# Two new tables for a fused attention, expert and convolution kernel: one for the order of its work, one for the engine of each step

## The chip, the cores and the metric

The kernel runs on one core of a Trainium2 chip. The metric is device time in microseconds (us), from one launch to its end. The core has TensorE (matmuls, written PE in the profile, with its weight loads as PEld), VectorE (DVE), ScalarE (ACT), GpSimd (POOL) and SyncE (SP), which here only issues DMA transfers.

## The reference

Three layers follow each other, on a batch of 4 with 576 positions. Local attention has 8 heads of 64; beside a band of 7 neighbours, each head attends over positions pooled by 4. A layer of 4 experts with causal attention follows, of which every token takes the best 2. Last is a gated convolution.

```python
# attention: q, k, v of shape (4, 8, 576, 64)
out_d = sm_attn(mean of q by 4, mean of k by 4, mean of v by 4)   # 144 x 144 scores
out_up = np.repeat(out_d, 4, axis=2)
scores = scale * q @ k.T where abs(i - j) < 4, else -1e9
out = out_up + softmax(scores) @ v
# experts: x of shape (4, 576, 512)
topk, w = best 2 of x @ w_gate, softmax over them
for e in range(4):
    a = softmax(causal(scale * (x @ wq[e]) @ (x @ wk[e]).T))
    out += (gate of e) * (a @ (x @ wv[e]) @ wo[e])
# gated convolution
gate = sigmoid(sum over k of conv_w[k] * shifted(x, k))           # 5 taps
return (gate * (x @ w_val)) @ w_out
```

## The kernel before

All of the work is cut into **pieces**. A piece belongs to one engine, issues one or a few instructions there, and names the buffers that it reads and writes. There are 2773 numbered pieces, 321 of which fall away by a choice of engine; 636 of the rest are TensorE's, 810 VectorE's, 566 ScalarE's, 305 GpSimd's and 135 are transfers. For each of the 4 batches these come one after another:

- `attention(b)`: for each of 4 pairs of heads the loads `qt`, `kt`, `vw`, `v`; the sums by 4 that give `qd` and `kd` (lines 946 and 953); pooled scores (1083), transposes (1099) and values (1117); band scores (1142, 1148), transposes (1161, copied out to `pT` at 1168) and values (1183). `softmax` is shared by both: the largest of each row (1007), its scaling `mx` (1017), the exponentials on ScalarE with a read of their accumulator (1022) or without one and a sum on VectorE after it (1028 and 1042), a small step `sm` that adds an epsilon (1051, 1053 or 1055 by engine), the reciprocal (1059) and the product with it (1068, 1070). The pooled values are scaled to `od` (1125), their transposed weights are copied to `pdT` (1106). The result x is split into a high and a low half, `xh` (798) and `xl` (815).
- `project(b)`: products of x with `wvg` (values `vE` and gate logits) and `wqk`, each as three matmuls of halves, all on lines 1228 to 1230. `experts(b)`: scores (1380, 1392), least score (1407, 1410), exponentials (1419), weighting by gate and sum (`weigh`, 1484 to 1520, where `rf` at 1510 is the product of two columns), transposes (1441, 1458), values (1552).
- `tail(b)`: the convolution (1600 to 1614) and the last products, again on lines 1228 to 1230, then scaling (1646, 1648) and the store.

Weights are loaded and split once; `w_val` and `w_out` come as 64-bit numbers and are decoded by lines 854 to 875, `w_val` is first multiplied by `wo` on TensorE (896). There are eight banks of PSUM (`ps`), shared by all stages, with a cap for each kind of use.

Nothing is issued in the order in which it is written down. `Plan.order()` walks through all pieces with costs and delays of its own and takes, for each engine that is free, the ready piece with the least **due time** for which there is room; the list that results is the program's order, fixed before it is compiled. The due time of a piece is `DUE[idx]`, with `idx` its number. A due time is a priority: the pieces that are ready are sorted by it, and no engine waits for a clock. Pieces of VectorE and GpSimd that are marked "port" are kept apart by the walk where a small delay allows it.

Which engine takes a step is a second table. Every step that more than one engine can do calls `pick` with its options, and the n-th call is answered by the n-th digit of `PICK`; a step that needs a helper on another engine (a copy out of PSUM for GpSimd, `rf` for ScalarE) gets it through `same`.

```python
def pick(self, name, *options):
    n = len(self.picks)
    k = min(int(PICK[n]), len(options) - 1) if n < len(PICK) else 0
...
p = Piece(engine, cost, late, (DUE[idx] if idx < len(DUE) else 0.0, idx), fn, k, size)
...
form = pick("a_" + key, *forms)             # ("act", "dve", ["none",] "pool", "half", "halfp")
tiny = pick("m_" + key, "act", "dve", "pool")
norm = pick("n_" + key, "act", "dve", "pool")
en = pick("pt_%s%d" % (key, c), "act", "dve")
```

Of the kernel before, what the change touches and what calls it, by code (L numbers as in the profile page):

```python
# [34 lines left out]
    0.3, 1.5, 0.7, 5.45, 1.6, 0, 0.15, 3.85, 3.6, 5.2, 4.58, 0.5, 6.19, 2, 3.88, 4.83, 0, 1, 9.28, 4.5,  # L35
    16.58, 3.52, 4.1, 6.05, 6.81, 0.5, 1.5, 6, 22.88, 5, 4.59, 5.08, 6.73, 7.22, 17.54, 18.54, 7.78,
    10.77, 11.82, 12.71, 12.29, 12.29, 14.5, 15.06, 15.35, 10.26, 11.2, 11.67, 11.89, 12.93, 14.04,
    14.63, 14.92, 16.62, 18.95, 18.53, 21.15, 22.48, 24.1, 12.93, 15.14, 15.84, 16.3, 16.3, 15.74,
    15.74, 16.3, 18.4, 19.77, 19.98, 15.54, 16.14, 16.14, 16.14, 16.3, 18.17, 19.37, 20.11, 20.98,
    21.27, 22.24, 23.25, 23.67, 24.3, 25.31, 25.72, 29.93, 30.84, 26.62, 27.82, 28.67, 29.8, 19.93,  # L40
    21.38, 22.41, 22.86, 22.88, 21.98, 21.98, 22.88, 24.96, 26.51, 26.86, 21.77, 22.37, 24.74, 22.81,
    22.37, 22.37, 22.81, 26.84, 27.4, 27.62, 28.69, 30.31, 30.41, 31.47, 32.48, 32.71, 33.81, 34.55,
    32.6, 35.41, 36.28, 37.2, 14.58, 16.08, 25.52, 29.42, 29.92, 19, 19.57, 22.52, 23.1, 21.38, 21.88,
    26.02, 33.48, 32.48, 26.15, 28.09, 27.07, 28.76, 38.08, 39.1, 25.08, 26.61, 27.49, 28.05, 27.82,
    27.2, 27.2, 27.82, 30.15, 32.11, 32.82, 27, 29.09, 30.66, 29.47, 27.6, 27.6, 29.47, 33.14, 33.4,
    33.62, 30.15, 31.59, 32.53, 33, 32.99, 34.03, 35.12, 36.22, 36.51, 32.2, 33.65, 34.31, 34.31, 35.7,
    36.42, 37.11, 37.42, 39.01, 40.64, 40.64, 43.37, 45.19, 45.36, 41.49, 42.74, 43.77, 44.96, 46.38,
    46.38, 47.01, 47.83, 46.38, 46.81, 47.39, 47.9, 34.03, 36.31, 37.91, 38.37, 38.41, 36.91, 36.91,
    39.9, 40.54, 41.15, 41.44, 36.71, 38.34, 38.81, 42.74, 37.31, 37.31, 44.12, 44.72, 45.59, 45.88,
    47.39, 48.66, 49.08, 49.87, 50.88, 51.19, 52.95, 53.68, 50.88, 50.88, 51.49, 51.88, 8.78, 16.41,  # L50
    16.83, 2.5, 7.96, 8.58, 4, 14.11, 14.72, 2, 7.58, 8.04, 23.38, 32.18, 34.17, 3, 8.93, 9.66, 22.38,
    29.18, 30, 15.08, 19.59, 20.38, 0, 6.42, 6.65, 6.88, 6.19, 5.5, 3.5, 10.65, 11.27, 11.42, 11.89,
    12.43, 13.81, 14.7, 18.02, 17.08, 15.58, 21.3, 21.85, 22.17, 22.9, 23.64, 25.02, 27.4, 25.97, 35.97,
    26.52, 39.99, 39.44, 41.24, 41.71, 42.79, 44.52, 50.65, 48.22, 62.46, 68.35, 72.56, 73.44, 73.47,
    74.01, 74.55, 75.98, 76.87, 79.31, 78.06, 0, 79.68, 80.5, 0, 81.49, 25.02, 31.29, 36.67, 28.92,
    38.23, 39.56, 91.07, 95.14, 95.28, 95.87, 96.51, 97.05, 98.35, 98.89, 98.73, 103.73, 104.59, 104.68,
    105.49, 106.54, 108.62, 110.24, 111.36, 45.41, 54.53, 55.08, 55.3, 56.23, 56.77, 58.25, 59.13,
    59.78, 59.13, 63.3, 63.85, 64.07, 64.78, 65.52, 67.02, 70.22, 70.96, 76.87, 81.7, 82.25, 82.63,
    84.21, 85.88, 87.59, 90.08, 91.52, 65.82, 66.18, 66.54, 66.9, 68.83, 68.15, 61.71, 62.07, 63.23,
    65.46, 66.35, 67.23, 57.48, 57.84, 58.2, 58.56, 60.29, 61.81, 53.46, 53.82, 54.54, 55.79, 56.81,  # L60
    60.56, 31.01, 38.28, 49.42, 54.18, 56.96, 54.82, 69.17, 69.57, 68.61, 69.91, 71.18, 71.73, 69.39,
    69.77, 72.45, 73.28, 73.82, 74.35, 74.87, 75.46, 80.78, 86.85, 69.38, 72.38, 72.73, 73.09, 73.99,
    74.54, 67.77, 68.23, 68.58, 69.73, 70.76, 70.32, 71.4, 73.44, 73.8, 74.15, 74.51, 75.65, 77.73,
    62.43, 63.59, 63.95, 65, 65.69, 65.69, 66.69, 35.55, 40.41, 52.92, 55.34, 59.18, 59.75, 58.94,
    59.51, 56.57, 57.15, 68.94, 70.09, 70.53, 71.83, 73.12, 72.61, 75.06, 54.9, 56.15, 56.59, 57.03,
    59.74, 62.55, 60.61, 62.88, 60.01, 62.31, 60.28, 60.83, 61.27, 62.79, 64.72, 64.4, 66.76, 7.44,
    7.33, 75.07, 76.67, 77.37, 76.94, 77.71, 78.06, 78.66, 78.55, 79.15, 79.82, 80.28, 80.55, 81.28,
    80.55, 81.83, 80.55, 81.43, 80.55, 82.35, 84.81, 86.38, 86.94, 89.84, 91.58, 92.29, 94.55, 95.43,
    99.19, 81.02, 82.36, 82.87, 82.09, 83.22, 83.81, 86.47, 85.07, 87.06, 87.75, 88.6, 88.88, 89.98,
    89.28, 90.6, 88.88, 90.96, 88.88, 89.22, 92.83, 94, 93.62, 94.92, 96.19, 96.19, 96.85, 97.13, 98,  # L70
    87.32, 88.67, 91, 89.38, 91.73, 94.37, 95, 95.27, 96.2, 95.27, 97.18, 98.5, 99.23, 99.31, 91.95,
    93.13, 94.48, 93.87, 95.52, 97.22, 99.77, 100.05, 103.44, 100.05, 101.53, 106.64, 109.82, 107.8,
    93.33, 96.78, 95.07, 98.53, 99.11, 99.6, 101.15, 104.61, 105.42, 105.83, 106.13, 107.27, 108.59,
    110.76, 113.29, 117.58, 117.19, 118.22, 111.81, 114.29, 116.07, 113.17, 116.63, 117.9, 119.75,
    120.02, 120.76, 120.02, 120.12, 125.38, 127.44, 126.58, 116.85, 117.91, 119.34, 118.65, 120, 121.41,
    121.93, 122.23, 124.79, 122.13, 124.17, 128.2, 129.16, 128.95, 118.11, 122.42, 119.38, 123.13,
    123.62, 126.11, 126.96, 127.71, 128.18, 128.46, 128.46, 129.82, 130.39, 131.42, 133.4, 135.96,
    135.96, 136.76, 32.98, 33.98, 40.59, 54.73, 61.46, 42.03, 43.17, 45.21, 45.72, 34.97, 35.47, 40.09,
    60.96, 61.96, 46.71, 47.61, 49.91, 50.48, 51.61, 52.74, 46.15, 48.26, 48.85, 49.2, 49.2, 48.85,
    48.85, 49.2, 51.29, 52.61, 53.33, 49.51, 50.11, 51.07, 50.56, 50.11, 50.11, 50.56, 53.19, 54.92,  # L80
    58.55, 51.61, 54.04, 54.69, 57.22, 55.02, 55.02, 60.22, 61.1, 62.84, 53.53, 54.56, 55.63, 54.89,
    54.89, 61.19, 61.72, 62.28, 64.3, 65.23, 65.84, 75.86, 77.3, 77.51, 67.26, 69.88, 70.2, 77.83,
    78.83, 78.95, 80.31, 82.86, 78.83, 79.38, 79.93, 80.8, 58.92, 60.08, 60.68, 60.68, 60.68, 61.32,
    61.92, 63.12, 65.04, 65.75, 66.04, 61.91, 63.2, 68, 63.67, 62.51, 62.51, 63.67, 70.62, 71.09, 72.2,
    80.27, 81.01, 81.35, 81.92, 82.93, 83.38, 84.3, 85, 82.93, 83.08, 83.92, 87.12, 48.12, 47.62, 54.23,
    78.83, 79.33, 57.39, 60.48, 55.04, 56.01, 59.96, 60.46, 53.73, 82.93, 90.57, 64.41, 64.98, 68.25,
    68.81, 61.02, 77, 70.97, 72.77, 75.58, 76.04, 76.05, 76.05, 77.97, 78.46, 79.24, 72.25, 73.03,
    74.25, 73.37, 73.37, 75.85, 77.2, 78.17, 83.58, 84.55, 85.47, 86.19, 88.31, 91.56, 78.61, 80.75,
    82.8, 83.27, 83.56, 81.35, 81.35, 85.98, 86.92, 87.41, 87.7, 80.35, 81.15, 84.59, 81.48, 80.95,
    80.95, 81.48, 86.99, 87.5, 88.89, 91.08, 92.56, 92.71, 93.95, 95.15, 95.44, 96.46, 97.23, 95.15,  # L90
    96.2, 96.84, 98.35, 88.42, 90.56, 91.16, 91.16, 91.16, 91.91, 92.9, 94.6, 96.85, 97.51, 97.8, 91.18,
    91.78, 91.78, 91.78, 92.31, 93.26, 97.6, 99.11, 99.84, 100.7, 102.31, 103.05, 103.39, 104.34,
    105.35, 105.93, 106.8, 107.4, 105.45, 105.91, 107.78, 110.42, 97.26, 99.82, 100.44, 100.41, 101.05,
    100.41, 101.84, 100.41, 102.63, 100.41, 103.82, 105.14, 103.63, 103.98, 106.69, 107.49, 108.42,
    96.42, 99, 100.08, 99.69, 100.66, 99.69, 101.45, 99.69, 102.24, 99.69, 103.03, 104.28, 105.93,
    106.28, 107.03, 108.28, 109.26, 107.6, 108.06, 109.88, 109.53, 110.46, 108.65, 111.84, 111.08,
    112.6, 108.91, 113.29, 114.12, 109.84, 110.56, 114.89, 115.77, 116.29, 95.96, 99.46, 101.63, 100.79,
    102.3, 100.05, 103.42, 100.05, 104.21, 100.05, 105.02, 105.69, 105.12, 105.57, 106.36, 107.18,
    108.08, 119.93, 121, 121.71, 122.06, 123.64, 127.92, 120.64, 121.35, 122.9, 123.25, 123.91, 124.39,
    118.51, 118.87, 119.22, 119.58, 120.16, 134.13, 117.66, 120.29, 126.69, 127.14, 127.81, 139.32,  # L100
    137.86, 138.3, 138.98, 138.98, 139.61, 138.98, 140.2, 138.98, 140.79, 138.98, 141.38, 144.24,
    146.75, 151.2, 152.12, 152.72, 153.41, 130.16, 138.75, 141.12, 139.43, 141.84, 139.43, 142.43,
    139.43, 144.18, 140.72, 145.44, 146.6, 154.55, 154.99, 155.72, 156.65, 157.73, 139.56, 140.01,
# [1609 lines left out]
```

## Time and profile before

| what | value |
|---|---|
| median of 3 runs | 355.61 us (353.96 to 356.92) |
| the profiled execution | 357.07 us |
| its span, first to last instruction | 355.4 us |
| instructions | 11539 |
| mean granted clock of TensorE | 0.974 |
| bytes moved | 31.70 MB, 89 GB/s over the span |

The profile is of one execution. Its span lies within its time, and what is left of the time is ahead of the first instruction and behind the last. Busy times are unions of an engine's instructions. [...]

### The profile page before, as it was taken

The numbers are of one execution on the slowest core, as the hardware profiler recorded it, in microseconds if no ns is written. First come the engines' busy times: TensorE is split into PE (matmuls) and PEld (weight loads), VectorE is DVE, ScalarE is ACT, GpSimd is POOL, SyncE is SP. The second block draws the span as 40 slices with busy tenths as digits, with TensorE's granted clock in tenths as the row PEclk, the third lists the DMA queues.
The fourth block names the chain that finished last, engine by engine and source line by source line (L and its number), as shares of the span: only waits on it lengthen the run. The fifth ranks groups of instructions, "written<-read, shape, count | busy, mean of one in ns | idle before, by whom it ended". The sixth has DMA issues, their size and how long they took to land.

```text
span 355.4 us, 11539 instructions
## 1 busy us (share of the span) xinstructions
PE 332.9 (94%) x4360; PEld 290.8 (82%) x4360; DVE 297.4 (84%) x921; ACT 257.8 (73%) x923; POOL 204.7 (58%) x325
## 2 busy tenths in 40 slices
PE   0697899998999999999999999999999999999996
PEld 0464679876698898999898897998998899997896
DVE  6898998899999899988989786898887668799572
ACT  3778968689888987688786797466765565688462
POOL 7357867559879852477978432384673036444070
PEclk9999589997899999999999999999999999999999
DMA  7979948519431344236222110101000100001022
GB/s 264 258 217 236 235 137 184 155 61 195 110 85 50 91 123 113 52 107 169 65 91 68 50 51 2 39 4 70 9 0 5 44 0 17 0 4 57 15 65 74
DMA packets 26279, 31.70 MB, mean 89 GB/s; under 512 B 2672, under 2 KB 18032, under 8 KB 26224
## 3 DMA queue, kind: packets, MB, share of 16 engines
q1 hardware_dynamic: 26224, 30.97, 32.4%
q8 instruction: 34, 0.56, 0.7%
q14 instruction: 21, 0.17, 0.2%
HBM read 26.24 MB, written 4.72 MB: 87 GB/s over the span
## 4 chain that ended last, share of the span: by engine, by line
PE 81%; DVE 9%; POOL 4%; ACT 3%; issue 2%; POOLq 0%; DVEq 0%
PE ps L1228 19%; PE ps L1229 17%; PE ps L1230 17%; PE ps L1552 7%; PE ps L1380 5%; PE ps L1441 3%; PE ps L1183 2%; PE ps L1148 2%; PE ps L896 2%; PE ps L1117 1%; PE ps L1161 1%; PE ps L1083 1%; DVE mx L1007 1%; ACT p L1022 1%; PE ps L1099 1%
## 5 line engine op out<-in xcount | busy, mean ns | idle before, releaser
L1419 ACT ACTIVATE pe<-ps,mmin 128x128 f32<-128x128 f32 (+4 forms) x80 | 41.9, 527 | 15.3 <-DVE mmin L1410 10.0
L1612 POOL TENSOR_TENSOR row<-row,row 128x256 f32<-128x256 f32 (+1 forms) x40 | 32.0, 804 | 33.0 <-ACT row L1607 18.4
L1614 DVE SCALAR_TENSOR_TENSOR row<-ps,cw,row 128x320 f32<-128x320 f32 (+1 forms) x88 | 43.3, 513 | 6.2 <-ACT row L1600 4.3
L1228 PE MATMUL ps<-gh,wout_h 128*128 128x256 f32 (+1 forms) x128 | 39.3, 307 | 0.5 <-DVE pT L1168 0.5
L1230 PE MATMUL ps<-xh,wqk_l 128*128 128x256 f32 (+1 forms) x128 | 37.8, 295 | 2.1 <-POOL wqk_l L815 2.1
L1228 PE MATMUL ps<-xh,wqk_h 128*128 128x256 f32 (+1 forms) x128 | 39.1, 306 | 0.6 <-DVE vE L790 0.3
L1229 PE MATMUL ps<-gl,wout_h 128*128 128x256 f32 (+1 forms) x128 | 37.8, 295 | 0.0
L1229 PE MATMUL ps<-xl,wqk_h 128*128 128x256 f32 (+1 forms) x128 | 37.8, 295 | 0.0
L1230 PE MATMUL ps<-gh,wout_l 128*128 128x256 f32 (+1 forms) x128 | 37.7, 294 | 0.0
L1552 PE MATMUL ps<-mp,vE 128*64 128x320 f32 (+4 forms) x224 | 27.0, 374 | 0.0
L1230 PEld LDWEIGHTS ps<-xh,wqk_l 128*128 128x128 f32 x128 | 24.2, 189 | 2.3 <-POOL wqk_l L815 2.3
L1228 PEld LDWEIGHTS ps<-gh,wout_h 128*128 128x128 f32 x128 | 24.1, 188 | 2.5 <-POOL gl L815 0.8
L1228 PEld LDWEIGHTS ps<-xh,wqk_h 128*128 128x128 f32 x128 | 24.1, 189 | 2.2 <-DVE vE L790 0.6
L1520 POOL TENSOR_SCALAR pe<-pe,rs,gw 128x128 f32<-128x128 f32 (+3 forms) x31 | 21.0, 683 | 7.8 <-DVE mmin L1415 4.9
L1007 DVE TENSOR_REDUCE mx<-ps 128x5 f32<-128x320 f32 (+1 forms) x48 | 23.7, 519 | 1.1 <-PE ps L1148 0.6
L1229 PEld LDWEIGHTS ps<-gl,wout_h 128*128 128x128 f32 x128 | 24.1, 188 | 0.2 <-POOL gl L815 0.2
L1229 PEld LDWEIGHTS ps<-xl,wqk_h 128*128 128x128 f32 x128 | 24.2, 189 | 0.0
L1230 PEld LDWEIGHTS ps<-gh,wout_l 128*128 128x128 f32 x128 | 24.1, 188 | 0.0
L1228 PE MATMUL ps<-wvg_h,xh 128*128 128x260 f32 (+1 forms) x80 | 23.5, 293 | 0.6 <-POOL xh L798 0.6
L1552 PEld LDWEIGHTS ps<-mp,vE 128*64 128x64 f32 (+1 forms) x224 | 14.2, 138 | 11.9 <-issue 3.9
L1230 PE MATMUL ps<-wvg_h,xl 128*128 128x260 f32 (+1 forms) x80 | 22.7, 284 | 1.0 <-DVE xl L815 1.0
L1229 PE MATMUL ps<-wvg_l,xh 128*128 128x260 f32 (+1 forms) x80 | 22.6, 282 | 0.0
(231 smaller groups left out, 1208.8 us busy)
## 6 DMA issues: line engine op xcount, KB each, us to landing
qt<-in_qT_dram SPq DMA_DIRECT2D x16, 288.0 KB, 3.7
kt<-in_kT_dram SPq DMA_DIRECT2D x16, 288.0 KB, 4.4
v<-in_vx_dram SPq DMA_DIRECT2D x16, 288.0 KB, 5.3
vw<-in_vx_dram SPq DMA_DIRECT2D x16, 192.0 KB, 4.1
out_dram<-o SPq DMA_DIRECT2D x16, 160.0 KB, 1.8
raw<-in_w_val_dram SPq DMA_DIRECT2D x4, 512.0 KB, 5.1
vw<-in_vx_dram SPq DMA_DIRECT2D x16, 128.0 KB, 3.9
raw<-in_w_out_dram SPq DMA_DIRECT2D x4, 512.0 KB, 3.5
```

The lines of the kernel that those rows point to most:

```text
L896: nc.tensor.matmul(pw[m].t, t.t[:, m * P:(m + 1) * P], f.t, start=(c == 0), stop=(c == KC - 1))
L1007: nc.vector.tensor_reduce(out=mx.t[:n, :g, 1], in_=sv(), op=ALU.max, axis=AX.X)
L1228: nc.tensor.matmul(p, ah, bh, start=first, stop=False)
L1229: nc.tensor.matmul(p, ah, bl, start=False, stop=False)
L1230: nc.tensor.matmul(p, al, bh, start=False, stop=last)
L1380: nc.tensor.matmul(s.t[:, o:o + P * (t + 1)], a.t[r, P * t:P * t + P], z.t[r, :P * (t + 1)], start=(k == 0 and t == T[0]), stop=(k == 2 an ...
L1419: nc.scalar.activation(pe.t[:, off + c0:off + c1], s.t[:, o:o + c1 - c0], AF.Exp, bias=m.t[:, 0:1], scale=-1.0, accum_out=sums.t[:, a:a + ...
L1441: nc.tensor.transpose(pt.t[:, i:i + 64], pe.t[r, j * P:(j + 1) * P], ident[r, r])
L1520: ENG[en].tensor_scalar(v, v, x, y, op0=ALU.mult, op1=ALU.mult)
L1552: nc.tensor.matmul(av.t[64 * e:64 * e + 64, z:n], vE.t[:kr, j, 2 * pr + e, :], pT.t[:kr, e, k0:k0 + n - z], start=(j == 0), stop=(j == Tl))
L1612: nc.gpsimd.tensor_add(g.t[:, :nn], g.t[:, :nn], g2.t[:, :nn])
L1614: nc.vector.scalar_tensor_tensor(g.t[:, :nn], x2.t[:, k:k + nn], cw.t[:, m, k:k + 1], g.t[:, :nn], op0=ALU.mult, op1=ALU.add)
```

## The change

Only the two tables change. `DUE` has 2773 entries before and after, so that every piece keeps its number and gets another priority. `PICK` has 1008 digits before and after, and 443 of them differ. The functions that make the pieces, `Plan.order()` and its costs, and all parameters stay. [...] The first and the last lines of `DUE` stand for the rest of it.

```diff
--- before.py
+++ after.py
@@ -32,238 +32,239 @@
 DUE = (
-    0.3, 1.5, 0.7, 5.45, 1.6, 0, 0.15, 3.85, 3.6, 5.2, 4.58, 0.5, 6.19, 2, 3.88, 4.83, 0, 1, 9.28, 4.5,
-    16.58, 3.52, 4.1, 6.05, 6.81, 0.5, 1.5, 6, 22.88, 5, 4.59, 5.08, 6.73, 7.22, 17.54, 18.54, 7.78,
...
-    343.71, 340.39, 343.49, 346.58, 347.02, 347.7, 348.24, 341.72, 343.04, 344.37, 344.81, 345.49,
-    346.02, 340.83, 342.6, 343.93, 345.25, 345.93, 346.53, 339.95, 342.16, 345.7, 346.14, 346.81, 347.35,
+    0.3, 1.8, 0.7, 5.35, 0, 0.5, 0.65, 1.6, 5.95, 6.65, 1.85, 0.8, 6.19, 0, 1.9, 4.15, 0, 1, 6.5, 4.5,
+    16.95, 3.52, 4.64, 4.59, 6.2, 1.5, 2, 5, 21.14, 7, 5.66, 6.39, 6.74, 7.23, 16.12, 17.39, 7.65, 9.7,
...
+    338.9, 340.67, 343.63, 344.23, 344.81, 341.99, 343.32, 344.65, 345.98, 346.65, 347.3, 341.55,
+    343.76, 344.21, 345.53, 346.2, 346.8, 342.44, 342.88, 345.09, 346.42, 347.09, 347.8, 341.11, 346.86,
+    347.3, 347.75, 348.42, 348.96,
 )


 PICK = (
-    "011100000001230000010112021100012002032101000120010100100011231130040010001000000150042211001021"
-    "212000102110110000002121012101010100110000111000010000010000001111000000000100111111120211000001"
-    "001011102000101100222011001010001001003203201021101111010210012000120002102100100101110222121110"
-    "400100010010012202220000012000000100000110110110000000100000000001000011200000010000100011111000"
-    "100111001110010100101010010010101012110112122001002000101101201012011112010001011110110111322002"
-    "100132251111101121202220000010010111111010421420222020000000001121212221000110011001210001210111"
-    "110000200000010020000021000021000021101000101100010001110000110010010110011011001001210101111021"
-    "101011220000110011111211012211001010100101010120222130210011011100110140052211001011110100111152"
-    "130201102011010000012132101101011110001021110010101100010010001111110100002101110001000000110110"
-    "110100011101010010111011000010100000011022112010011100010022101001002110002000120100010000001110"
-    "110010002110010011010000210000211111200100000010"
+    "010100000032210001001202021100012012030100000100000100000031231142040001010101100152040201021021"
+    "010111002110112000002101210110010000010111010001001100000010001010000011000100111111110011000001"
+    "000210001000021100212101011010111101000010014200220100000210212204120002102100000001112000021000"
+    "420010000010012202120000002100102100000000100100110100100000010001000001211100200000101110100010"
+    "011000001100110101110010111101102111100002021000002111101200100012000110000010100111111111022322"
+    "010141150201101120202322001010111101000111202400020221000100001110210221111010210000201000201100"
+    "011000210010001001010001000020010000010111110100100010111010101010110110100000010111200110110022"
+    "201000201102001000110211112010020000100011101000240130042001001001100030041210000001111111101142"
+    "240042141101100012010141050110111120100120000111010021011101010101102001112011000100002000011001"
+    "000110111001111111100011111100100000110022002110111001001010100110101001102201110100011000110010"
+    "000000000100102101100100210010211100010100000110"
 )
```

## Rows read from the trace of the kernel before

**Rows 1.** The page: busy time of each engine, share of the span, instructions.

```profile
PE 332.9 (94%) x4360; PEld 290.8 (82%) x4360; DVE 297.4 (84%) x921; ACT 257.8 (73%) x923; POOL 204.7 (58%) x325
```

**Rows 2.** Windows: length; busy PE, PEld, DVE, ACT, POOL (instructions); clock; DMA share; GB/s.

```profile
0.00:50.00 50.00, 33.57 (x586) 23.87 (x587) 43.28 (x118) 34.37 (x147) 32.52 (x68) 0.90 0.89 237
50.00:100.00 50.00, 47.65 (x685) 39.37 (x685) 46.05 (x155) 42.68 (x176) 38.28 (x52) 0.93 0.54 132
100.00:150.00 50.00, 50.00 (x670) 45.08 (x670) 45.96 (x138) 41.62 (x147) 31.62 (x48) 1.00 0.34 87
...
300.00:355.40 55.40, 52.19 (x457) 46.75 (x456) 38.55 (x112) 33.21 (x91) 19.67 (x28) 0.99 0.11 37
```

**Rows 3.** Waits of TensorE: for whom, us in total, times, longest; last row after 95 us.

```profile
PE ps L1083 <- POOL kd L953: 8.1, 1, 8.1
PE ps L896 <- DVE o L875: 3.2, 1, 3.2
PE ps L1230 <- POOL wqk_l L815: 2.1, 1, 2.1
...
PE ps L1228 <- DVE pT L1168: 0.5, 1, 0.5
```

**Rows 4.** The window from 94 to 352 us, columns as in rows 2.

```profile
94.00:352.00 258.00, 257.47 (x3181) 232.66 (x3176) 214.00 (x673) 185.99 (x625) 138.54 (x215) 1.00 0.18 52
```

**Rows 5.** Timeline of TensorE near 108 us: start us, us, engine, line, operation.

```profile
107.14 0.28 PE L1229 MATMUL ps<-al,wv_h 128*128 128x256 f32 x1
107.26 0.28 PE L1230 MATMUL ps<-ah,wv_l 128*128 128x256 f32 x1
107.47 0.71 PE L1441 MATMUL ps<-ident,pe 64*128 64x64 f32 x16
...
108.42 0.39 PE L1228 MATMUL ps<-ah,wo_h 128*128 128x260 f32 x1
108.64 0.28 PE L1229 MATMUL ps<-al,wo_h 128*128 128x260 f32 x1
```

**Rows 6.** The page: the chain that ended last, shares of the span.

```profile
PE 81%; DVE 9%; POOL 4%; ACT 3%; issue 2%; POOLq 0%; DVEq 0%
```

**Rows 7.** Windows ahead of and in both half-clock stretches, columns as in rows 2.

```profile
26.60:36.84 10.24, 7.02 (x131) 4.40 (x129) 9.09 (x27) 8.24 (x41) 8.17 (x13) 1.00 1.04 236
...
36.84:47.08 10.24, 9.09 (x156) 7.51 (x154) 9.64 (x19) 7.96 (x29) 8.47 (x10) 0.50 0.84 220
...
84.63:91.45 6.82, 6.72 (x93) 5.02 (x93) 6.37 (x23) 6.82 (x33) 6.51 (x10) 0.50 0.69 120
```

**Rows 8.** Groups by shape, VectorE and ScalarE: busy us, mean ns; then idle before.

```profile
L1042 DVE TENSOR_REDUCE sm<-p 128x5 f32<-128x320 f32 x19 | 9.0, 475 | 1.0 <-ACT p L1037 0.8 <-ACT p L1028 0.2
L1168 DVE COPY pT<-ps 128x348 f32<-128x348 f32 x15 | 7.4, 508 | 0.3 <-PE ps L1161 0.3
...
L1106 DVE COPY pdT<-ps 112x432 f32<-112x432 f32 x10 | 5.9, 596 | 0.0
L946 DVE TENSOR_TENSOR row<-kt 128x288 f32<-128x288 f32 x9 | 4.3, 475 | 0.0
L790 DVE COPY vE<-ps 128x256 f32<-128x256 f32 x9 | 3.8, 417 | 0.1
L1125 DVE TENSOR_SCALAR od<-ps 128x144 f32<-128x144 f32 x7 | 2.0, 299 | 0.2
...
L1022 ACT ACTIVATION_READ_ACCUMULATOR p<-ps,mx 128x1 f32 x65 | 14.7, 225 | 0.0
...
L1168 ACT COPY pT<-ps 128x348 f32<-128x348 f32 x17 | 7.3, 461 | 2.7 <-PE ps L1161 2.7
```

**Rows 9.** Instructions of three lines: count, then min/median/max ns, first and last start.

```profile
L1059 DVE RECIPROCAL sm<-sm x48: 147/178/192, 14.4 to 243.5; 128x5 f32<-128x5 f32 x32, 128x3 f32<-128x3 f32 x16
...
L1053 DVE TENSOR_REDUCE sm<-sm x11: 124/149/166, 14.3 to 243.3; 128x5 f32<-128x10 f32 x7, 128x3 f32<-128x6 f32 x4
...
L1510 DVE TENSOR_TENSOR rf<-rs,gw x15: 119/159/686, 89.4 to 329.4; 128x1 f32<-128x1 f32 x15
```

426 rows, old and new, of the table DUE are left out of this document.

## Prediction

> **What bounds the kernel now.** I read the page's busy times first, and they mislead: TensorE looks busy for 94% of the span and VectorE for 84%, as if there were one limit throughout [rows 1]. The windows of 50 us split it. In the first two, TensorE has 16.4 and 2.4 us of idle time, while VectorE is busy for 43.28 and 46.05 of 50 us and the DMA engines for 0.89 and 0.54 of theirs; from 100 us on TensorE has none, and the other engines have more and more of it [rows 2]. The waits of TensorE alone, asked for once from 20 to 95 us and once from 95 to 352 us, give the date of the turn: after 95 us a single wait of 0.5 us stands, and the long ones (2.1 us for the low half of a weight) lie ahead of it; the two longest of all are 8.1 us at the start and 3.2 us for the first decoded weight [rows 3]. The window from 94 to 352 us has 257.47 us of TensorE in 258.00 [rows 4]. A busy TensorE need not be at its peak, so its pace is read from the timeline: matmuls of 256 columns start 0.12 us apart, without a gap, also where a group of transposes stands between them [rows 5].
>
> So the time is three parts: about 94 us in which TensorE is fed too thinly, 258 us that are its own instructions one behind another, and some 3 us at the end in which the last results are scaled and stored (it is busy for 52.19 of the last 55.40 us) [rows 2]. The instructions of the 258 us are the same products whatever their order. **What a new order can win lies in the first 94 us**: how much TensorE work gets done there. The chain of waits says who holds it: outside TensorE it is VectorE 9%, GpSimd 4% and ScalarE 3%, which is 32, 14 and 11 us of 355.4, and since TensorE alone fills the time after 95 us, nearly all of it lies ahead [rows 6]. [...]
>
> **The change part by part.** No instruction of the program is written anew; 443 of the 1008 choices of engine differ, and the order. The digit at place n answers the n-th call of pick(), so each changed digit is a named step, and a mean duration from the groups by shape prices it on either engine.
>
> (a) Work per engine. Over the whole run VectorE loses 6.1 us, ScalarE gains 3.0 and GpSimd 0.5. That would be too coarse a sum, since it counts VectorE where TensorE hides it. Of the steps that stood before 100 us, VectorE loses 3.5 us, ScalarE gains 1.3, GpSimd loses 0.4. The main terms for VectorE: four copies of pT go to ScalarE (4 x 508 ns = 2.03 us), three of od (3 x 299 = 0.90), two of vE (2 x 417 = 0.83), one of pdT (0.60); against them two more sums of exponentials (475 ns for a wide one, the pooled one is longer: 1.07 us in all) and two more pair sums (2 x 475 = 0.95); the rest comes to -1.2 in small items [rows 8]. For ScalarE the four pT copies cost 4 x 461 = 1.84 us, but eight exponentials lose their accumulator read (8 x 225 = 1.8 us) because VectorE now sums them [rows 8]. How much of the 3.5 us reaches TensorE? None, if the loads hold this stage: the DMA share is 1.04 just ahead of 36.84 us [rows 7]. All of it, if VectorE does: 46.05 of 50 us. By the chain, a third (32 of some 95 us), 1.2 us. I take half, **-1.8 us**, because from 50 us on VectorE is the fullest engine but for TensorE and the DMA engines have room; the ends are 0 and -3.5. ScalarE and GpSimd come to about nothing: ScalarE gains 2.5 us before 50 us, where it is busy for 34.37 of 50, and loses 1.2 us in the next 50 [rows 2]: 11% of chain on +1.3 us is **+0.1 us**.
>
> (b) The order on TensorE. Sorted by their due times, 88 of its 636 pieces keep their place and 32 move by over 20 places; the stages stay where they were. The number of changes between kinds of matmul grows from 147 to 151. One such change costs what the start-to-start times show: 0.21 us from the last 256-column matmul to the first transpose, and the group behind starts late in like manner, against 0.12 us within a run [rows 5], so 0.1 us each, **+0.4 us**, and nothing hides it in the 258 us.
>
> (c) The queue of loads. 28 of 135 keep their place. At the start q0, q1, k0, k1 become q0, k0, q1, k1, and the first pair sum of k0 moves from GpSimd to VectorE (475 ns there) [rows 8]. TensorE's first matmul needs kd, the end of that line [rows 3]; but the sums of both pairs now queue on VectorE, and k1 lands last as before. Bounds -0.3 and +0.3 us, I take 0. Among the later loads those of the second weight and of the next batch are exchanged; the cover is the long lead that they have, and what it costs where that is gone is a wait such as the 2.1 us one.
>
> [...]
>
> Sum: -1.8 + 0.1 + 0.4 = -1.3 us. The profiled execution took 357.07 us, 1.7 us more than its span of 355.4, and the median of the three runs is 355.61; the same difference gives 355.8 for the one and **354.3 us** for the other, -0.4%.
>
> **The rivals.** First, nothing is gained: the loads hold the first 40 us and the freed VectorE time waits for them. For it: the DMA share of 1.04. Against it: the share is 0.54 from 50 to 100 us. It gives 355.6 + 0.4 = 356.0 us. [...]
>
> Second, faster by over 1%: the half-clock stretch at 84.63 us goes, because with VectorE freed TensorE has no thin stretch ahead of it. It would give 354.3 - 3.4 = 350.9 us; with all of the 3.5 us, 349.2. Against it: nothing in the tables aims at that place, and the pooled transposes and a band stage move up there by 2 to 4 us of due time, which can thin it as well.
>
> Third, slower: TensorE is fed too thinly before 47.08 us and the first half-clock stretch lasts once more as long. ScalarE has 2.5 us more to do before 50 us, and most of what TensorE works on there passes through it first. Another 10.24 us at half clock cost up to 5.1 us, and with no gain of VectorE that is 356.0 + 5.1 = 361.1; another 6.82 us give 359.4. It decides from the point at which the rise at 47.08 us comes later than about 54 us. Against it: ScalarE keeps over a quarter of that window idle.
>
> **How the numbers follow.** Forecast 354.3, from 352.3 with (a) and (c) at their low ends to 355, where the next case begins: 0.42. Nothing gained, 355 to 357: 0.21. The clock stretch gone, 349 to 352: 0.21. Slower, 357.5 to 361: 0.16. About 1%, 3.6 us, is what a measurement of this kernel can tell from no change, its three runs lying 3 us apart. Faster by more (under 352.0): the third case and little else, 0.24. Slower by more (over 359.2): most of the last, 0.13. The rest, 0.63. The range leaves out a tenth at each end: 349.6 to 359.4.
>
> **What the changed profile would show.** TensorE's only waits after 95 us under 1 us, and its window from there to the end as long as before to 1 us: then the frame is right. VectorE busy 2 to 4 us less before 100 us, and TensorE's last wait some 2 us sooner: (a). Two stretches of 0.50 clock, as long as now: the forecast; one, or three, the second or third rival. [...] It is wrong if TensorE waits in the middle of the run, which the means can't show: then the new order has starved a stage that was covered.

## The result, and the profile after

The changed kernel takes 358.43 us, the kernel before 354.85 us, medians of 14 runs each on the same chips. The ratio is 1.0095, with a 95% interval from 1.0069 to 1.0122: about 3.4 us slower, where the forecast was 1.3 us faster. The profiled execution took 357.8 us, its span 356.1 us. In all listings below a line number of the changed kernel is one higher than in the kernel before, and a few more where an experiment adds lines.

The page, busy times, clock in 40 slices of the span, and shares of the chain:

```profile
PE 332.9 (94%) x4360; PEld 290.2 (81%) x4360; DVE 292.2 (82%) x901; ACT 262.2 (74%) x929; POOL 206.8 (58%) x328
...
PEclk9889699999699999999999999999999999999999
...
PE 84%; POOL 5%; DVE 4%; ACT 3%; DMA 2%; issue 1%; SPq 1%; POOLq 0%; ACTq 0%; DVEq 0%
```

VectorE does 5.2 us less than in [rows 1] and its share of the chain falls from 9 to 4% [rows 6]. The windows (columns as in [rows 2]):

```profile
0.00:50.00 50.00, 33.08 (x590) 23.24 (x590) 40.67 (x116) 36.13 (x153) 35.67 (x72) 0.86 0.87 234
50.00:100.00 50.00, 47.10 (x681) 39.18 (x681) 45.15 (x150) 43.49 (x171) 37.96 (x52) 0.93 0.49 130
100.00:150.00 50.00, 50.00 (x669) 44.45 (x669) 44.48 (x131) 38.90 (x139) 37.76 (x54) 1.00 0.32 89
300.00:356.10 56.10, 52.76 (x461) 47.30 (x460) 38.81 (x116) 30.79 (x85) 21.27 (x32) 1.00 0.10 34
...
94.00:352.00 258.00, 257.86 (x3164) 232.47 (x3157) 211.11 (x654) 186.49 (x623) 137.29 (x213) 1.00 0.18 51
```

VectorE is busy 2.6 and 0.9 us less in the first two windows than in [rows 2], 3.5 in all, which is the sum of part (a). (A second profile of each kernel gives 84.1 us of VectorE in the first 100 us for 88.0, so the sum holds to some 1.5 us.) From 94 us on TensorE is as full as in [rows 4]. So the frame holds, the work moved as forecast, and yet the time went the other way. TensorE's waits (all of the run):

```profile
PE ps L1084 <- POOL kd L954: 7.0, 1, 7.0
PE ps L897 <- DVE o L876: 3.9, 1, 3.9
PE ps L1162 <- ACT p L1069: 1.6, 2, 1.4
...
PE ps L1231 <- POOL wqk_l L816: 0.9, 1, 0.9
```

Three of them answer to [rows 3]: 7.0 for 8.1 us, 3.9 for 3.2 and 0.9 for 2.1; after 95 us none is left. The third is new: the transposes of a band softmax (line 1162) wait 1.4 us for ScalarE's weighting of the rows by the reciprocal of their sum (line 1069). Here is where it lies, in windows cut at that wait and at the clock:

```profile
80.00:86.75 6.75, 5.58 (x136) 4.04 (x134) 6.57 (x22) 6.62 (x31) 5.93 (x9) 1.00 0.87 192
86.75:88.18 1.43, 0.00 (x2) 0.01 (x2) 1.43 (x6) 1.43 (x8) 1.43 (x3) 1.00 0.70 186
88.18:89.26 1.08, 0.88 (x15) 0.64 (x16) 1.04 (x6) 1.08 (x5) 1.08 (x3) 1.00 0.92 270
89.26:96.09 6.83, 6.73 (x79) 4.74 (x77) 5.24 (x19) 4.94 (x18) 6.61 (x10) 0.51 0.04 14
96.09:100.00 3.91, 3.91 (x31) 3.48 (x30) 3.87 (x16) 3.91 (x14) 2.27 (x4) 0.99 0.17 50
```

TensorE is idle for 1.43 us; 1.2 us after it goes on, the granted clock falls to half for 6.83 us. The row to read is the fourth: TensorE is busy for 6.73 of 6.83 us there, while VectorE and ScalarE, which fed it almost without a pause just before, are down to 5.24 and 4.94. GpSimd is still at 6.61, but the chain of work from 84 to 97 us runs through TensorE alone from 90.22 us on: TensorE holds the others. In the kernel before, the second half-clock stretch has VectorE at 6.37 and ScalarE at 6.82 of 6.82 us [rows 7]: there the vector engines are as full as TensorE (6.72).

Why ScalarE is late with line 1069 stands in its timeline (start us, us, engine, line, operation, tiles):

```profile
84.74 0.62 ACT L799 CAST wout_h<-o 128x512 fp32r<-128x512 f32 x1
85.27 0.47 ACT L1420 ACTIVATE pe<-ps,mmin 128x256 f32<-128x256 f32 x1
...
85.73 0.46 ACT L1420 ACTIVATE pe<-ps,mmin 128x256 f32<-128x256 f32 x1
...
86.18 1.29 ACT L1069 ACTIVATE p<-p,sm 128x64 f32<-128x64 f32 x5
87.37 0.27 ACT L1126 ACTIVATE od<-ps 128x144 f32<-128x144 f32 x1
87.54 1.30 ACT L1069 ACTIVATE p<-p,sm 128x64 f32<-128x64 f32 x5
```

It has no pause here, and the cast of a weight and one od copy, which the new tables put there, stand ahead of the second weighting.

To see where time is won and lost along the run, I counted the TensorE work done by a given time: every matmul weighs the mean start-to-start time that its line and shape take after 100 us in the kernel before. The table gives how many us of such work each execution is ahead of the profiled one of before (rows that name an edit are experiments, below; added matmuls weigh nothing). Each row is one execution, and that of the kernel before took 357.07 us, well over its median of 354.85, so the rows of one kernel are to be compared with those of the other and not with zero.

| execution | by 85 us | by 100 us | by 350 us |
|---|---|---|---|
| before, a second profile | +0.3 | +2.1 | +1.5 |
| before, gap filled | +0.3 | +0.8 | +0.6 |
| before, early gaps filled too | -0.2 | +0.8 | 0.0 |
| changed | +2.2 | +0.2 | -0.8 |
| changed, a second profile | +1.3 | -1.7 | -2.8 |
| changed, same matmuls elsewhere | +2.5 | +0.3 | -2.6 |
| changed, real work moved | +2.2 | +0.9 | -0.3 |
| changed, gap filled | +1.1 | +1.4 | +0.3 |
| changed, early gaps filled too | +1.9 | +2.2 | +1.2 |

The changed kernel is ahead at 85 us, by about what (a) had promised. Unless its gap is filled it loses 1 to 3 us of that work by 100 us, where the other executions of the kernel before gain 0.5 to 1.8. Up to 350 us it loses a further 1 us.

### The profile page after: what moved, and what is told of

Its sections match the earlier page's. It is cut to its first block, busy times and chain, and to the rows that moved or that the text cites. A ratio compares the mean times of both kernels' runs of the same rounds, so it can differ in the third digit from the quotient of the medians.

```text
span 356.1 us, 11532 instructions
## 1 busy us (share of the span) xinstructions
PE 332.9 (94%) x4360; PEld 290.2 (81%) x4360; DVE 292.2 (82%) x901; ACT 262.2 (74%) x929; POOL 206.8 (58%) x328
## 4 chain that ended last, share of the span: by engine, by line
PE 84%; POOL 5%; DVE 4%; ACT 3%; DMA 2%; issue 1%; SPq 1%; POOLq 0%; ACTq 0%; DVEq 0%
PE ps L1229 19%; PE ps L1230 17%; PE ps L1231 17%; PE ps L1553 7%; PE ps L1381 5%; PE ps L1442 3%; PE ps L1184 3%; PE ps L897 2%; PE ps L1149 2%; DMA raw<-in_w_val_dram 2%; PE ps L1162 2%; PE ps L1118 2%; PE ps L1084 2%; PE ps L1100 1%; POOL row L1613 1%
## 5 line engine op out<-in xcount | busy, mean ns | idle before, releaser
L1613 POOL TENSOR_TENSOR row<-row,row 128x256 f32<-128x256 f32 (+1 forms) x38 | 30.7, 812 | 34.3 <-DVE row L1615 19.6
L1615 DVE SCALAR_TENSOR_TENSOR row<-ps,cw,row 128x320 f32<-128x320 f32 (+1 forms) x90 | 44.4, 512 | 7.3 <-ACT row L1608 2.9
L1229 PE MATMUL ps<-xh,wqk_h 128*128 128x320 f32 (+1 forms) x128 | 39.0, 305 | 0.1
L1231 PE MATMUL ps<-xh,wqk_l 128*128 128x320 f32 (+1 forms) x128 | 37.8, 296 | 0.9 <-POOL wqk_l L816 0.9
L1230 PE MATMUL ps<-xl,wqk_h 128*128 128x320 f32 (+1 forms) x128 | 37.8, 295 | 0.0
L791 ACT COPY mp<-ps 128x384 f32<-128x384 f32 (+2 forms) x43 | 19.9, 504 | 9.7 <-PE ps L1442 5.4
L1521 POOL TENSOR_SCALAR pe<-pe,rs,gw 128x384 f32<-128x384 f32 (+3 forms) x29 | 18.8, 651 | 12.2 <-DVE rs L1492 6.9
```

Of the source, the lines that this page charges most:

```text
L791: (nc.scalar.copy if eng == "act" else ENG[eng].tensor_copy)(out(), src())
L1229: nc.tensor.matmul(p, ah, bh, start=first, stop=False)
L1230: nc.tensor.matmul(p, ah, bl, start=False, stop=False)
L1231: nc.tensor.matmul(p, al, bh, start=False, stop=last)
L1521: ENG[en].tensor_scalar(v, v, x, y, op0=ALU.mult, op1=ALU.mult)
L1613: nc.gpsimd.tensor_add(g.t[:, :nn], g.t[:, :nn], g2.t[:, :nn])
```

## The experiments

Three theories stood at the start. **A**: the loss is TensorE's clock, which falls to half over work that TensorE itself limits. **B**: it is the late supply by another engine. **C**: it lies in the later stages, where TensorE is always busy. All ratios are to the kernel before, on the same chip, from five rounds.

**The two kernels again, for their spread.** No edit.

> The kernel before, unchanged, as a second profile and as a measure of how far two executions of one program lie apart. Every theory expects a ratio of 1.000 within 0.3%. They differ in what its clock shows: if the change costs time through TensorE's clock (theory A), these runs have a mean granted clock higher than the 0.971 to 0.976 that most runs after the change show, by 0.005 or more, which is 1.7 us of 355; if it costs time through late supply (theory B: an engine hands TensorE its operands later, whatever the clock), the clocks are alike, 0.971 to 0.976, and the spans some 3 us shorter all the same.

> The changed kernel, unchanged, as a second profile. Every theory expects a ratio between 1.007 and 1.012. Theory A expects half-clock stretches of 17 us or more before 100 us again, and the last wait of TensorE in this profile later than in the new one of before by as much as the stretches are longer, halved. Theory B expects TensorE to wait again for ScalarE's scaled softmax rows between 85 and 90 us, by 1 to 2 us.

Measured: 0.9988 [0.9972, 1.0005] and 1.0092 [1.0060, 1.0125]. The windows of this second profile of before, cut at its half-clock stretch:

```profile
80.00:85.70 5.70, 4.64 (x113) 3.77 (x111) 5.53 (x20) 5.70 (x26) 5.62 (x9) 1.00 0.87 199
85.70:89.10 3.40, 3.40 (x62) 2.42 (x57) 3.33 (x14) 3.40 (x17) 3.23 (x6) 0.50 0.66 142
89.10:95.00 5.90, 5.71 (x95) 4.63 (x96) 5.83 (x21) 5.90 (x21) 5.82 (x7) 1.00 0.49 130
```

VectorE and ScalarE go on at 3.33 and 3.40 of 3.40 us while the clock is at half: the place is as in the first profile, the length isn't. The second profile of the changed kernel has its stretch at the same work, from 89.0 us, and 10.24 us long; it took 359.69 us. There TensorE waits 1.4 us again for line 1069.

Of the signs that were set, B's came true: over these runs the mean granted clock is 0.965 to 0.981 for the kernel before, 0.975 in the mean, and 0.960 to 0.980 for the changed one, 0.971 in the mean, so nearly alike, while the spans are some 3 us apart. A had asked for at least 17 us of half clock before 100 us in the changed kernel, which holds (27.3 us in this profile, 20.5 in the first), and for a higher clock of the kernel before by 0.005 or more, which doesn't. If A is right, it isn't by the length of the stretches but by what lies under them.

The executions on record say how much length matters. Among 99 of the kernel before, one more us at half clock, as its mean granted clock gives it, goes with 0.05 us more time (to 0.04 either way); among 70 of the changed kernel and of its variants with added matmuls or moved steps, with 0.16 us (to 0.05). Where TensorE alone sets the pace it would be nearly 0.5, an estimate from the profile of the changed kernel: matmuls of 288 columns start 0.24 us apart at half clock (at 92.93 and 93.17 us) and 0.13 us apart at full clock (at 97.02 and 97.15 us). This is a correlation, over stretches wherever they lie.

**Early and late halves of the tables.**

```diff
 # early_new; late_new takes the other halves
+DUE = DUE_NEW[:833] + DUE[833:]
+PICK = PICK_NEW[:316] + PICK[316:]
```

> The new tables for the pieces up to the second batch's attention (the first 833 pieces, the first 316 choices), the old ones for all others. Since TensorE has no wait after 97 us in either kernel, theories A and B both expect the whole loss here: a ratio of 1.007 to 1.012. Theory C, that the loss is in the order or the engines of the later stages, expects 1.000 within 0.003.

> The old tables for the first 833 pieces and 316 choices, the new ones for the rest. Theories A and B expect 1.000 within 0.003, theory C 1.007 to 1.012.

Measured: 1.0140 [1.0109, 1.0172] and 1.0085 [1.0054, 1.0116]. The second is what C expected, the first is above what A and B did. But both halves are slower, by more together than the whole, so they don't add up. The late half is 2.8 us ahead by the count at 100 us and loses 4.0 from there to 350 us; the early half loses 2.7 us there, though its tables for that part are mostly the old ones; the whole loses 1. So a seam seems to cost by itself, and nothing follows for C.

**One table without the other.**

In the kernel before, one table is replaced:

```diff
+DUE = DUE_NEW      # due_only: new order, old engines
+PICK = PICK_NEW    # pick_only: old order, new engines
```

> The new due times with the old engine choices. Theory A (the time goes to TensorE's clock: the new order lets TensorE run out of work at 86.75 us and the clock falls over the dense work behind it): the order alone does it, ratio 1.005 to 1.010, a half-clock stretch of 6.8 us or more beginning at 88 to 91 us. Theory B (a late supply by the engine that the new choices load, ScalarE): the old choices take 1.2 us off ScalarE between 80 and 90 us, the wait for the scaled softmax rows falls under 0.7 us and the ratio to 1.000 to 1.005. Theory C (what is lost lies in the later stages): at 100 us it is as far as the kernel before, and loses over 1 us behind it.

> The old due times with the new engine choices. Theory A: the gap of TensorE lies where the old order put it, so 0.997 to 1.003. Theory B: ScalarE is loaded more and the softmax rows come late here too, 1.004 to 1.010, with a wait of over 1 us for ScalarE between 80 and 95 us. Theory C: a loss of over 1 us between 100 and 350 us.

Measured: 1.1019 [1.0987, 1.1051] and 1.0424 [1.0397, 1.0451]. Every range was missed. (Of the other signs one came true, C's loss after 100 us with the new engines alone; by the count it is 9.6 us, far more than C was made for.) An order is fitted to the engines that its steps run on; taken apart, the tables say nothing on what they do together.

**Fill the gap.** Ten matmuls run ahead of the transposes that wait, into the bank that these overwrite.

```diff
+FILL = {'12': 10}
...
     def band_values(key, ld, ps, od, down, xh, xl):
...
         def _():
+            for _ in range(FILL.get(key, 0)):
+                nc.tensor.matmul(pts[0].t[:, :LATER], identb, later, start=True, stop=True)
```

> The changed kernel with ten matmuls that fill TensorE's gap at 86.75 to 88.18 us (they write a bank that the next transposes overwrite). Theory A: the half-clock stretch that begins at 89.3 us is gone or half as long, 1.7 to 3.4 us come back, ratio 1.000 to 1.004. Theory B and theory C: TensorE computes nothing useful earlier, so the ratio stays at 1.008 to 1.011.

Measured: 1.0035 [1.0013, 1.0057]. So 0.60% or 2.1 us of the 3.4 come back by adding work (by the two intervals, to 1.2 us either way). Its windows, cut as above, though this execution comes 1.0 us later to the same place (its ten matmuls start at 87.73 us):

```profile
86.75:88.18 1.43, 1.34 (x14) 0.83 (x13) 1.43 (x4) 1.43 (x9) 1.43 (x3) 1.00 0.53 90
88.18:89.26 1.08, 1.08 (x10) 0.60 (x8) 1.08 (x5) 1.08 (x6) 1.08 (x2) 1.00 0.48 132
89.26:96.09 6.83, 6.11 (x96) 4.25 (x96) 6.54 (x24) 6.56 (x24) 6.83 (x10) 1.00 0.25 78
```

No fall of the clock here, and over its 12 runs the mean granted clock is 0.983, for 0.971 of the changed kernel. In the last row TensorE does 96 matmuls for 79, and VectorE and ScalarE are busy 6.54 and 6.56 us for 5.24 and 4.94. This is what A expected, and neither B nor C. The late supply itself is as it was, so its own 1.4 us stays in what is left.

**The same ten matmuls where there is no gap**, ahead of a later pair's transposes; in the profile they start at 131.7 us, not near 150.

```diff
-FILL = {'12': 10}
+FILL = {'20': 10}
```

> The changed kernel with the same ten matmuls ahead of a pair's transposes near 150 us, where TensorE has no gap, instead of in the gap at 86.75 us. Theory of the clock: nothing comes back, the stretch at 89 us stays, and ten matmuls of about 0.13 us are added to a full TensorE: 1.3 us or 0.4% more than the changed kernel, 1.011 to 1.015. Rival (the ten matmuls help by something other than filling the gap): below 1.008.

Measured: 1.0150 [1.0122, 1.0177]. The added work costs, and nothing comes back; the stretch is there (length, busy times and clock as above):

```profile
85.00:90.00 5.00, 3.03 (x39) 1.82 (x35) 4.93 (x19) 4.81 (x21) 5.00 (x7) 0.96 0.65 166
90.00:95.00 5.00, 5.00 (x55) 3.42 (x57) 3.47 (x12) 3.92 (x14) 5.00 (x7) 0.50 0.02 6
```

So it is the filled gap, and not the matmuls as such, that helps. One added matmul takes 0.136 us (first at 87.73, last at 88.96 us: 1.23 us for nine), ten 1.36 us or 0.4%; 0.55% was measured, to 0.4% either way.

**The same for the kernel before**, whose own gap, waits of 0.3 and 0.7 us, lies ahead of its stretch at 84.6 us.

```diff
+FILL = {'m001': 8}     # ahead of the transposes of the first experts' rows
```

> The kernel before with eight matmuls that fill its own gap of TensorE ahead of the half-clock stretch at 84.6 us (before the pooled transposes of batch 0; they write a bank that the transposes overwrite). If the loss of the changed kernel is the place of this stretch (in the kernel before it lies where the vector engines set the pace, in the changed one over dense work of TensorE), the kernel before gains less than the changed one did by the same means (0.6%): ratio 0.996 to 1.001. If fillers help the kernel before as much, 0.992 to 0.995, the clock costs both the same, and the loss of 0.9% is elsewhere.

Measured: 1.0003 [0.9976, 1.0031]. That lies in A's range, but it isn't A's test. In its profile the clock is full from 47 to 91 us and at half for 3.4 us from there, behind a wait of 1.2 us at 89.3 us: a shorter stretch came later instead. Over its 12 runs the mean granted clock is 0.976, for 0.975 of the kernel before on the same chip. So this run doesn't price that stretch; the 0.05 us for each us, above, does. With both gaps filled 1.0035 stands against 1.0003: 0.3% or 1.1 us, to 1.3 us either way, so it isn't told from nothing.

**The early gaps filled too**, ahead of the first long stretch at 36 to 47 us.

```diff
+FILL = {'12': 10, 'q010': 7, 'd02': 12, '02': 5}   # after_fill3
+FILL = {'m001': 8, 'q010': 15, 'v041': 18}         # before_fill3
```

> The changed kernel with the ten matmuls at 87 us and 24 more in the gaps of 33 to 40 us. Theory of the clock: no half-clock stretch between 30 and 100 us, and 2 to 4 us less than with the ten alone (1.0035): 0.992 to 0.998, and if the order itself is as good as the old one, the same as the kernel before with its gaps filled, within 0.3%. Rival (the new order itself is slower, by the later stages): 0.3 to 0.6% over the kernel before with its gaps filled.

> The kernel before with the eight matmuls at 84 us and 33 more in the gaps of 33 to 38 us, ahead of the first long half-clock stretch (36.8 to 47 us, in which TensorE is nearly always busy and does half of what it does at full clock). Theory of the clock: that stretch gets shorter or goes, and 2 to 4 us come back: 0.988 to 0.996. Rival (the vector engines limit there too, or the stretch only comes later): 0.997 to 1.004.

Measured: 1.0050 [1.0020, 1.0079] and 1.0104 [1.0057, 1.0152]. The plan was for 24 and 33 more matmuls, but the key 'q010' answers to two pieces: the profiles have 31 and 48 more, 41 and 56 in all, and the second group of 'q010' stands among full matmuls (the lines give count, min/median/max ns, first and last start; then TensorE's timeline there):

```profile
L1338 PE MATMUL ps<-later,identb x7: 299/299/311, 67.6 to 68.5; 128*128 128x320 bf16 x7
...
L1335 PE MATMUL ps<-later,identb x15: 296/299/299, 67.5 to 69.4; 128*128 128x320 bf16 x15
...
67.49 0.31 PE L1238 MATMUL ps<-xh,wqk_l 128*128 128x320 f32 x1
67.64 1.12 PE L1338 MATMUL ps<-later,identb 128*128 128x320 bf16 x7
68.50 0.39 PE L1236 MATMUL ps<-xh,wqk_h 128*128 128x256 f32 x1
```

Windows of the changed kernel with the ten alone, and with all:

```profile
30.00:40.00 10.00, 6.30 (x119) 4.36 (x113) 7.76 (x18) 7.82 (x34) 9.76 (x13) 0.85 1.06 236
40.00:50.00 10.00, 9.85 (x181) 7.37 (x181) 7.22 (x18) 5.95 (x23) 6.89 (x10) 0.64 0.61 152
```

```profile
30.00:40.00 10.00, 7.21 (x131) 5.27 (x130) 7.88 (x18) 7.39 (x31) 9.01 (x13) 1.00 1.08 223
40.00:50.00 10.00, 9.10 (x198) 6.40 (x200) 8.64 (x21) 7.38 (x34) 8.13 (x12) 1.00 0.70 197
```

The clock is full in these windows, and nothing is won in the time. The misplaced matmuls are part of that. At 0.136 us each, seven take 1.0 us and fifteen 2.0 us of a full TensorE. By the count the changed kernel with all is 1.7 us ahead of the one with the ten alone at 60 us and 0.8 at 70, 85 and 100: what it gives back, it gives back there. The kernel before falls from +1.6 at 60 us to -0.4 at 70; so of the 1% that it is slower (3.7 us) some 2 us have a cause, the rest has none that I know. Less that 1.0 us, 1.0050 would be 1.0023, against 1.0035 with the ten alone: a gain of 0.4 us, to 1.3 us either way, and not the 2 to 4 us that were expected. No version here beats the kernel before.

**Take the late supply away.** The cast of wout was to go behind the two weightings, and one pdT copy goes back to VectorE.

```diff
+DUE = DUE[:357] + (91.0,) + DUE[358:]
+PICK = PICK[:285] + "10" + PICK[287:]
```

> The changed kernel with two edits between 82 and 89 us: the cast of the third output projection's piece goes behind two norms on ScalarE, and one pair's copy of transposed rows goes back to VectorE. Theory B: the wait of TensorE for the scaled softmax rows falls from 1.4 us to under 0.5, and with it the time to 1.000 to 1.004. Theory A: the same if the gap closes, but then the half-clock stretch at 89 us must be gone too; if the gap closes and the stretch stays, A is wrong. Theory C: 1.008 to 1.011 whatever becomes of the gap.

Measured: 1.0151 [1.0124, 1.0178]. The wait for line 1069 is gone from TensorE's list, which now begins, from 80 to 100 us, with another one; and the windows show the clock at half from 86.7 us on:

```profile
PE ps L1446 <- POOL pe L1525: 2.1, 1, 2.1
```

```profile
85.00:90.00 5.00, 4.47 (x85) 3.27 (x83) 5.00 (x19) 4.20 (x22) 4.83 (x7) 0.67 0.68 163
90.00:95.00 5.00, 2.94 (x30) 1.92 (x28) 4.86 (x13) 4.75 (x19) 5.00 (x7) 0.50 0.42 128
95.00:100.00 5.00, 5.00 (x63) 3.75 (x65) 2.89 (x9) 2.16 (x7) 4.84 (x9) 0.50 0.15 43
```

But the supply wasn't taken away. The pdT copy moved; the cast still stands ahead of both weightings, for a due time is only a priority, and ScalarE is idle for 0.80 us ahead of it:

```profile
87.74 0.62 ACT L803 CAST wout_h<-o 128x512 fp32r<-128x512 f32 x1 [0.80 <-DVE o L880]
...
89.17 1.30 ACT L1073 ACTIVATE p<-p,sm 128x64 f32<-128x64 f32 x5
...
90.54 1.30 ACT L1073 ACTIVATE p<-p,sm 128x64 f32<-128x64 f32 x5
```

The clock falls at 86.7 us, behind a wait of 0.8 us and at the start of one of 0.5 us, and TensorE, at half clock, comes to the transposes at 91.54 us, later than the weighting. The 2.1 us wait for GpSimd comes after the fall, from 92.9 us. With the same two steps and a full clock there the old wait is back, in the first of the next two runs:

```profile
PE ps L1167 <- ACT p L1074: 1.6, 2, 1.4
```

So B has not been tested by this. Then its gaps were filled, first in the wrong place:

```diff
+FILL = {'m001': 8, 'm002': 16}    # norms_fill
+FILL = {'12': 10, 'm011': 18}     # norms_fill2
```

> The kernel with the two moved steps between 82 and 89 us (1.0151; its half-clock stretch lasts from 86.7 to 100.4 us) with matmuls in the gaps of TensorE that it has: eight ahead of the pooled transposes at 83.8 us and 16 ahead of those at 92.4 us. Theory of the clock: the stretch of 13.7 us goes or is under half as long, and 2 to 4.5 us come back: 1.002 to 1.009. Rival (the late supply costs by itself, and the clock only goes with it): 1.012 to 1.018.

> The variant with the two moved steps again, now with its matmuls where its gaps are: ten ahead of the transposes of the batch's third pair (1.4 us of waiting) and 18 ahead of the pooled transposes of pair 1 (2.6 us of waiting at 90.1 to 92.8 us). Theory of the clock: the half-clock stretch of 10 to 14 us behind them goes or is under half as long, and 2 to 4.5 us of the variant's 5.4 come back: 1.002 to 1.009. Rival (the late supply costs by itself, the clock only goes with it): 1.012 to 1.018.

Measured: 1.0208 [1.0179, 1.0238] and 1.0109 [1.0066, 1.0152]. In the first, 16 matmuls ran from 97.3 us on, where TensorE has no gap, and a wait of 2.4 us stayed: it says again that such matmuls cost where there is no gap. In the second the profile shows no half clock between 44 and 354 us,

```profile
85.00:90.00 5.00, 4.80 (x42) 3.16 (x43) 4.93 (x16) 5.00 (x21) 5.00 (x5) 1.00 0.48 132
90.00:95.00 5.00, 4.36 (x81) 3.08 (x78) 3.70 (x11) 2.77 (x10) 4.84 (x10) 1.00 0.15 43
```

and that execution took 357.18 us. It is the fastest of its seven, whose median is 358.67, against 360.44 without added matmuls. The ratio lies between the two theories' ranges, so it decides for neither; part of that variant's loss stays with its gaps filled.

**Real work in the gap.**

```diff
+DUE = DUE[:537] + (91.5,) + DUE[538:551] + (91.8,) + DUE[552:]
```

> The changed kernel with two groups of score matmuls of the mixture (batch 0, pair 0, third block, and the pieces of the next one) put ahead of the transposes that TensorE waits for at 86.75 us: real work in the gap in place of fillers. Theory of the clock: if they can run there, the gap shrinks under 0.7 us, the stretch at 89 us goes or is halved, and the ratio falls to 1.000 to 1.005. If they wait for a bank themselves, the transposes come later and the ratio is 1.009 to 1.014. If the gap goes and the stretch stays, the theory is wrong.

Measured: 1.0067 [1.0046, 1.0089], which decides nothing: the two groups of scores came to stand behind the transposes, not ahead (they start at 89.04 and 90.10 us), the wait is still 1.43 us and the half-clock stretch 6.83 us. A due time is only one of the conditions by which the order is made.

## Why the prediction was wrong

**The frame was right.** TensorE has no wait after 95 us and is as full from 94 us as before. Only the first 94 us and the kind of work behind them could matter. The time moved the other way and lies where the third rival stood, which I had given 0.16.

**(a) was right in work, and right in size up to 85 us.** VectorE lost the 3.5 us in the first pair of profiles; six executions of the changed order, with or without added matmuls, are 1.1 to 2.5 us ahead at 85 us, four of the old -0.2 to 0.3. The term was -1.8. That the lead comes from VectorE's saved work is likely and not shown by a run of its own.

**The step that failed is the one from there to the sum: that such a lead is kept, and that the clock costs nothing new.** I took the two half-clock stretches as given, "as long as now", with a price that hangs on their length alone, so the clock stands at nothing in the sum. But this lead of TensorE over the engines that feed it ran out: its next piece in the order, the transposes, had to wait for ScalarE's weighting, TensorE stood still for 1.43 us, and the clock fell over work that TensorE limits. Filling the gap gave back 2.1 us (0.60%, to 0.35% either way); the same matmuls elsewhere gave nothing. That much is shown. What late supply costs by itself, without the clock, is not: the run that was to take it away didn't.

**The third rival named the right mechanism at the wrong place.** It put a lasting half clock at 36.84 us and priced it at half its length. With that stretch gone the runs gain 0.4 us at best estimate, to 1.3 us either way (1.0050 against 1.0035, less the misplaced matmuls), and 0.05 to 0.16 us for each us at half clock would be 0.5 to 1.6 us for 10.24: far from 5.1 us. The same holds for the second rival: the stretch at 84.63 us, which I priced at 3.4 us, would be worth 0.3 us by the executions of the kernel before; the run that filled its gap can't say, since the clock then fell later. The point from which I let the third rival decide, a rise later than 54 us, wasn't reached (45.0 us), and the loss came all the same. The count of stretches that I proposed as its sign came true by luck: the changed profile has a third one, at 14.2 us, but the count of work at 25 us shows no loss from it.

No run shows the prices of the two rivals, 3.4 us for 6.82 us at half clock and 5.1 us for 10.24 us: they are my estimate, half of a stretch's length. For the 6.83 us at 89 us it would be 3.4 us as well. There filling the gap gave 2.1 us, to 1.2 us either way, and over all stretches the executions on record give 0.05 to 0.16 us for each us, not 0.5: the estimate is an upper end here, and the measurement decides.

**(b) was low, if anything.** From 100 to 350 us five executions of the changed kernel without and with filled gaps lose 0.9 to 1.2 us by the count, four of the kernel before 0 to 0.8: 0.7 us between the means, where the four added changes of kind were to cost 0.4. No run isolates it.

**(c) came to nothing, as said, but not within its bounds.** The first wait is 7.0 for 8.1 us, where I had allowed 0.3; the wait for the first decoded weight is 3.9 for 3.2 us, and the count is level at 15 us. Of the small steps (count, min/median/max ns) the reciprocal takes 145 to 193 ns, for 147 to 192, and rf, fewer, 299 ns at most, for 686 [rows 9]:

```profile
L1060 DVE RECIPROCAL sm<-sm x48: 145/178/193, 15.3 to 243.6; 128x5 f32<-128x5 f32 x32, 128x3 f32<-128x3 f32 x16
...
L1511 DVE TENSOR_TENSOR rf<-rs,gw x10: 146/148/299, 124.4 to 325.2; 128x1 f32<-128x1 f32 x10
```

In sum: of 3.4 us, 2.1 (to 1.2 either way) are the clock at 89 us (shown), some 0.7 the later stages (read from counts of single executions, cause not isolated), and the rest, less than the intervals can tell, is not placed; the wait of 1.43 us itself may be in it. And the lead of 1 to 2 us at 85 us is worth nothing even at full clock: with the gap filled the changed kernel isn't faster than the kernel before. That VectorE and ScalarE are nearly full between 85 and 100 us in both (14.5 and 14.7 of 15 us with the gap filled, 14.5 and 13.5 in the kernel before) would explain it; no run tests it.

## What to carry to other kernels

Where the pace passes from the vector engines to TensorE, look for the last gap of TensorE and for what runs in the half-clock stretch behind it. Here it cost time where VectorE and ScalarE had idle time in that stretch (busy for 5.24 and 4.94 of 6.83 us; filling the gap gave 2.1 us), and little, by the executions on record, where they were nearly full (6.37 and 6.82 of 6.82 us; 0.05 us for each us); that is one kernel, and by the best estimates a price by length alone was too high in every case.

To price the clock while the order is made isn't enough: `Plan.order()` raises a matmul's cost where it guesses a lowered clock (`cost *= 1 + slow / len(phases)`), and these tables leave the gap all the same. A few matmuls into a bank that is about to be overwritten are a quick test of what a gap costs. But look in the profile where an edit has landed before reading its time: in three of the runs here matmuls meant for a gap stand where TensorE has none, and one new due time left its step where it was. And two tables found together are not to be judged by halves.

## What the runs showed of the hardware

In the first profile of the changed kernel 1.43 us of idle TensorE, with waits of 0.2 us on either side, were followed by 6.83 us at half clock, in the second profile of the same program by 10.24 us. Shorter waits precede a fall as well: 0.3 and 0.7 us in the kernel before, followed by 6.83 us in one profile and 3.41 us in the other. The length alone doesn't give the time: these two profiles of the kernel before have 17.1 us at half clock each ahead of 100 us, and spans of 355.4 and 353.8 us. And a whole program can hold its clock, mean 0.995 with 41 matmuls more, and be no faster for it (1.0050, against 1.0035 with ten matmuls more and a mean of 0.985), though seven of these stand in the way of others.
